# Splitting the first loads, doing the first projections chunk by chunk, warming TensorE with zeros, and merging the last segment's two projections

## The chip, the cores and the metric

The kernel runs on one core of one Trainium2 chip. The metric is the device time of one execution in microseconds (us); lower is better. A profile's span is about 1.7 us shorter than the time of the same execution. Five engines run side by side, each with its own instruction stream in order: TensorE (PE; its weight loads are listed as PEld), VectorE (DVE), ScalarE (ACT), GpSimd (POOL) and SyncE (SP). "ACTq" and "SPq" are the queues through which ScalarE and SyncE issue DMA transfers.

## The reference, cut to what matters

```python
# x: [1, 2048, 512] in 4 segments of 512 rows; 32 heads of width 16; all weights bf16
g = sigmoid((x * gate_w).sum(-1))
# A: causal attention inside each segment, plus a memory M, z summed over the earlier ones
q, k, v = x @ wq, x @ wk, x @ wv
o = sig(beta) * (phi(q) @ M) / (phi(q) @ z) + (1 - sig(beta)) * softmax(q k^T / 4 + mask) @ v
a = o @ wo
# B: a gated MLP, inner width 1792
b = (gelu(x @ w_gate) * (x @ w_up)) @ w_down
out = g * a + (1 - g) * b
```

## The kernel before

x is loaded transposed (`xT`, four chunks `fc` of 128 columns, each a partition block). A product of 512 rows with 128 weight columns is four matmuls of 128x128 by 128x512, accumulated in one PSUM bank. A list scheduler inside the kernel, fed with guesses of durations and of when loads arrive (`ext`), fixes each engine's order when the kernel is built. Its numbers are guesses, not measurements.

The loads and the guesses of their arrival (ns):

```python
load_w(nc.scalar, wk, A_wk)                 # whole, 512 KB, on ScalarE's queue
load_x(0)                                   # 4 transposing DMAs on SyncE's queue
load_w(nc.scalar, wq, A_wq)
load_w(nc.scalar, wv, A_wv)
nc.scalar.dma_start(gw[:, :], ...)
load_w(nc.scalar, wga, B_w_gate)            # 1792 KB
nc.scalar.dma_start(beta8[:, :], ...)
for s in range(1, NSEG): load_x(s)
load_w(nc.sync, wup, B_w_up); load_w(nc.sync, wdn, B_w_down); load_w(nc.sync, wo, A_wo)
a_x = [ext(t) for t in (7000, 11000, 16000, 20000)]
a_wk, a_wq, a_wv, a_gw = ext(5500), ext(8500), ext(11500), ext(12000)
```

k, then q, of segment 0, bank after bank (two `gen` banks in turn):

```python
def mm_x(t, W, c0, s):
    for fc in range(FC):
        nc.tensor.matmul(t, lhsT=W[:, fc, c0:c0 + P], rhs=xT[:, fc, s * L:(s + 1) * L],
                         start=(fc == 0), stop=(fc == FC - 1))
...
for c in range(NCH): qk_group(0, c, "k", 10 + c, "DVE")
for c in range(NCH): qk_group(0, c, "q", 20 + c, "DVE")
for kt in range(KT): v_group(0, kt, 30 + kt, "DVE")
```

The end of the last segment: the MLP product (`dn`) of each of four row blocks goes through a bank into dead space of `G`; the attention product (`fin`) has banks of its own; VectorE adds the two into one of two `osb` buffers, which are stored:

```python
def down_group(s, qt, prio):
    first, prev, box = pieces(s, qt, prio, True, ...)       # 14 matmuls, one bank
    ... copy(e, G[:, 0, qt, :], box["t"][:, :])             # evicted by ACT or DVE
def final(h):                                               # h = 0, 1: two row blocks each
    ... proj_o(box["t"][:, i, :], 3, 2 * h + i, range(3), True)   # heads' chunks 0..2
    ... proj_o(box["t"][:, i, :], 3, 2 * h + i, [3], False)       # the last chunk
    ... nc.vector.tensor_add(bx["o"][:, :], box["t"][:, i, :], G[:, 0, 2 * h + i, :])
    ... store(s, 2 * h + i, bx["o"])
```

The softmax here doesn't subtract the row's maximum and nothing guards it: scores larger than these inputs give would overflow.

## Time and profile before

| | before |
|---|---|
| time, median of all 15 runs beside the change | 299.29 us (the first three alone: 299.54) |
| span of the profiled run | 297.7 us |
| TensorE busy | 275.7 us, 93% |
| first k matmul | 7.60 us |
| first attention logits (`lg`) | 84.7 us |
| start of the last `pv` matmul | 274.8 us |

From the page's second part (the span in 40 slices of 7.4 us; a digit is the busy share in tenths, PEclk the granted clock in tenths):

```profile
PE   0999999999999979999998999998999999999991
PEclk9999999999999999999999999999999999999998
GB/s 194 205 320 277 308 3 0 2 0 0 0 2 36 6 39 30 36 2 2 1 2 35 20 53 20 20 1 2 0 21 21 18 2 18 20 21 18 20 0 70
```

TensorE is idle in the first slice and nearly so in the last; in all others it is busy for seven tenths or more. So those two are where most time can be had without doing less work. Note the granted clock: it reads 9 in every slice but the last. The next view shows why that isn't the whole truth.

From the timeline of before, its first 23 us (start, duration, engine, line, operation, out<-in, shape, count, and in brackets the idle time ahead and what ended it):

```profile
7.60 6.17 PE L314 MATMUL k<-xT,wk 128*128 128x512 bf16 x16 [7.60 <-DMA xT<-in_A_x_dram]
7.80 0.44 ACTq L239 DMA_DIRECT2D wv<-in_A_wv_dram  x1
8.41 0.15 PEld L314 LDWEIGHTS <-wk 128*128 128x128 bf16 x1 [0.28 <-issue]
8.84 0.15 PEld L314 LDWEIGHTS <-wk 128*128 128x128 bf16 x1 [0.28 <-issue]
12.68 0.60 PEld L314 LDWEIGHTS <-wk 128*128 128x128 bf16 x3 [0.28 <-issue]
13.00 0.44 ACTq L239 DMA_DIRECT2D wga<-in_B_w_gate_dram  x1
13.66 3.01 PE L314 MATMUL q<-xT,wq 128*128 128x512 bf16 x12
14.33 1.28 ACT L378 ACT_TABLE_LOAD   x1 [14.33 <-DMA gw<-in_gate_w_dram]
17.73 3.78 PE L352 MATMUL v<-wv,xT 128*128 128x512 bf16 x16
22.28 10.09 PE L314 MATMUL gt<-xT,wga 128*128 128x512 bf16 x46
```

TensorE waits for x until 7.60. Then the weight loads, one per matmul, start 0.43 us apart (8.41, 8.84) until 12.68; from there three take 0.60 us together, and later matmuls of this shape come 0.216 us apart. The array runs at half speed for its first 5.1 us of work, and the PEclk row doesn't show it. `wga`, which the gate matmuls (`gt`) need, is only issued at 13.00: ScalarE's queue stands still between its issues. The view doesn't name the reason; `wv` left at 7.80, after `wq` had landed (1.27 + 5.9 = 7.2), and `wga` at 13.00, after `wv` had (7.80 + 4.5 = 12.3), which fits issues that wait for an earlier load but doesn't show it. ScalarE's first work of its own, a table load, starts at 14.33, when the last issue is done.

From the DMA view of before, the last figure being the time from issue to landing:

```profile
wga<-in_B_w_gate_dram ACTq DMA_DIRECT2D x1, 1792.0 KB, 7.5
wk<-in_A_wk_dram ACTq DMA_DIRECT2D x1, 512.0 KB, 4.3
```

The tail of before, from the timeline:

```profile
290.12 1.03 PE L752 MATMUL fin<-wo,xT 128*128 128x512 bf16 x4
290.81 1.29 DVE L817 TENSOR_TENSOR osb<-fin,G 128x512 bf16<-128x512 f32 x2 [12.42 <-PE fin L752]
291.53 3.45 SPq L757 DMA_DIRECT2D out_dram<-osb  x4
293.33 1.29 DVE L817 TENSOR_TENSOR osb<-fin,G 128x512 bf16<-128x512 f32 x2 [1.24 <-DMA out_dram<-osb]
```

The last matmul ends at 290.12 + 1.03 = 291.15; 6.55 us follow. Two adds wait 1.24 us for a store to give an `osb` buffer back.

Two lines, from the views of the tiles `lg` and `pv`, divide the span ("84.7 to 264.0" are the first and last start):

```profile
L496 PE MATMUL lg<-qT,kT x320: 213/278/386, 84.7 to 264.0; 16*128 16x256 bf16 x64, 16*128 16x128 bf16 x64, 16*128 16x512 bf16 x32
L545 PE MATMUL pv<-pT,vz x640: 218/272/393, 99.6 to 274.8; 128*32 128x256 bf16 x64, 128*32 128x128 bf16 x64, 128*32 128x512 bf16 x32
```

I call what lies before the first `lg` the start (84.7 us), what lies between it and the last `pv` the middle (190.1), and the rest the end (22.9).

### The profile page before, as it was taken

To read this page: it belongs to the slowest core of one execution; us is meant where nothing else is said; L and a number is where in the kernel's file an instruction comes from. 1 tells how busy PE (TensorE), PEld (TensorE's weight loads), DVE (VectorE), ACT (ScalarE), POOL (GpSimd) and SP (SyncE) were. 2 spreads that over 40 slices of the span, in tenths; PEclk is the share of its full clock that TensorE was granted. 3 is DMA by queue.
4 is the path that set the end of the run, shared out by engine and by line. 5 is a ranking of instruction groups with operands and counts; after the bars stand their busy time and mean duration, and the time that the engine had idled before them with its cause. 6 is when DMAs were issued, how large, how long until landed. Compare 5 with 4: busy or idle time off the path is not lost.

```text
span 297.7 us, 5661 instructions
## 1 busy us (share of the span) xinstructions
PE 275.7 (93%) x2297; PEld 117.6 (40%) x2297; DVE 203.2 (68%) x361; ACT 206.7 (69%) x224; POOL 126.1 (42%) x186
## 2 busy tenths in 40 slices
PE   0999999999999979999998999998999999999991
PEld 0344444444433434344334444433444434344440
DVE  0484465446567798987999788689977855867303
ACT  0007565443479997899998899999998989984110
POOL 7000000000007883974558687564755864663000
PEclk9999999999999999999999999999999999999998
DMA  7998900000001011100001020000000000000002
GB/s 194 205 320 277 308 3 0 2 0 0 0 2 36 6 39 30 36 2 2 1 2 35 20 53 20 20 1 2 0 21 21 18 2 18 20 21 18 20 0 70
DMA packets 23106, 13.74 MB, mean 46 GB/s; under 512 B 16168, under 2 KB 22056, under 8 KB 23080
## 3 DMA queue, kind: packets, MB, share of 16 engines
q1 hardware_dynamic: 20400, 9.97, 12.1%
q10 hardware_dynamic: 2680, 3.41, 3.7%
q8 instruction: 18, 0.29, 0.4%
q14 instruction: 8, 0.07, 0.1%
HBM read 7.60 MB, written 2.10 MB: 33 GB/s over the span
## 4 chain that ended last, share of the span: by engine, by line
PE 73%; DVE 21%; DMA 3%; issue 1%; ACT 0%; DVEq 0%
PE gt L314 16%; PE dn L747 15%; PE up L314 14%; PE lg L496 6%; PE pv L545 5%; PE k L314 4%; PE v L352 3%; PE dn L752 3%; PE q L314 3%; DVE T L563 2%; DMA xT<-in_A_x_dram 2%; DVE G L416 2%; DVE Nm L736 2%; DVE N L581 2%; DVE Tm L732 1%; DVE vz L178 1%
## 5 line engine op out<-in xcount | busy, mean ns | idle before, releaser
L517 ACT ACTIVATE pT<-lg 128x1024 bf16<-128x1024 f32 x160 | 153.5, 1028 | 12.9 <-PE lg L496 12.3
L526 POOL TENSOR_SCALAR_AFFINE_SELECT pT<-pT 128x512 bf16<-128x512 bf16 (+1 forms) x160 | 94.4, 601 | 139.3 <-ACT pT L517 138.7
L416 DVE TENSOR_TENSOR G<-up,G 128x512 bf16<-128x512 f32 x56 | 38.3, 687 | 28.4 <-PE up L314 28.3
L314 PE MATMUL up<-xT,wup 128*128 128x512 bf16 x224 | 56.0, 380 | 0.6 <-DVE G L416 0.4
L747 PE MATMUL dn<-wdn,G 128*128 128x512 bf16 x224 | 53.3, 380 | 0.1
L314 PE MATMUL gt<-xT,wga 128*128 128x512 bf16 x224 | 51.0, 379 | 0.0
L404 ACT ACTIVATE G<-gt 128x1024 bf16<-128x1024 f32 x28 | 28.7, 1023 | 30.3 <-PE gt L314 30.3
L314 PEld LDWEIGHTS <-wga 128*128 128x128 bf16 x224 | 21.9, 98 | 26.5
L747 PEld LDWEIGHTS <-G 128*128 128x128 bf16 x224 | 20.2, 98 | 25.6 <-issue 4.1
L314 PEld LDWEIGHTS <-wup 128*128 128x128 bf16 x224 | 20.0, 97 | 25.8 <-issue 5.6
L563 DVE STREAM_TRANSPOSE T<-pv 128x512 f32<-128x512 f32 x32 | 22.7, 711 | 10.3 <-PE pv L545 10.3
L407 DVE TENSOR_TENSOR G<-G,g1b 128x1024 bf16<-128x1024 bf16 x28 | 19.2, 687 | 13.7 <-ACT G L404 13.7
L545 PE MATMUL pv<-pT,vz 128*32 128x256 bf16 (+2 forms) x640 | 23.4, 275 | 3.0 <-POOL pT L526 1.8
L314 PE MATMUL k<-xT,wk 128*128 128x512 bf16 x64 | 18.1, 427 | 8.6 <-DMA xT<-in_A_x_dram 7.6
L496 PE MATMUL lg<-qT,kO 32*128 32x128 bf16 (+2 forms) x320 | 18.1, 272 | 0.0
L496 PE MATMUL lg<-qT,kT 16*128 16x256 bf16 (+2 forms) x320 | 17.9, 274 | 0.0
L314 PE MATMUL q<-xT,wq 128*128 128x512 bf16 x64 | 16.3, 380 | 0.8 <-DVE kT L178 0.5
L545 PEld LDWEIGHTS <-vz 128*32 128x32 bf16 x640 | 12.6, 97 | 11.1 <-DVE G L416 2.2
L352 PE MATMUL v<-wv,xT 128*128 128x512 bf16 x64 | 15.7, 379 | 1.0 <-DVE vz L178 0.5
L618 POOL TENSOR_TENSOR pkT<-E,Q 128x1024 bf16<-128x1024 bf16 x6 | 13.5, 2254 | 3.6 <-DVE E L614 2.1
L581 DVE TENSOR_TENSOR N<-T,r 128x512 bf16<-128x512 f32 x16 | 14.8, 926 | 0.3
L496 PEld LDWEIGHTS <-kT 16*128 16x128 bf16 x320 | 7.1, 92 | 19.6 <-issue 19.2
(78 smaller groups left out, 240.4 us busy)
## 6 DMA issues: line engine op xcount, KB each, us to landing
out_dram<-osb SPq DMA_DIRECT2D x16, 128.0 KB, 1.7
wga<-in_B_w_gate_dram ACTq DMA_DIRECT2D x1, 1792.0 KB, 7.5
wup<-in_B_w_up_dram SPq DMA_DIRECT2D x1, 1792.0 KB, 7.4
wdn<-in_B_w_down_dram SPq DMA_DIRECT2D x1, 1792.0 KB, 13.3
wk<-in_A_wk_dram ACTq DMA_DIRECT2D x1, 512.0 KB, 4.3
wq<-in_A_wq_dram ACTq DMA_DIRECT2D x1, 512.0 KB, 5.9
wv<-in_A_wv_dram ACTq DMA_DIRECT2D x1, 512.0 KB, 4.5
wo<-in_A_wo_dram SPq DMA_DIRECT2D x1, 512.0 KB, 14.1
```

The lines of the kernel that those rows point to most:

```text
L314: nc.tensor.matmul(t, lhsT=W[:, fc, c0:c0 + P], rhs=xT[:, fc, s * L:(s + 1) * L], start=(fc == 0), stop=(fc == FC - 1))
L352: nc.tensor.matmul(t[:, :], lhsT=xT[:, fc, s * L + kt * P:s * L + (kt + 1) * P], rhs=wv[:, fc, :], start=(fc == 0), stop=(fc == FC - 1))
L404: ge = evac("ACT", g, box, lambda e, t: nc.scalar.activation(dst, t[:, :, :], AF.Gelu_apprx_tanh), cost=960, ring="lg")
L407: GM[(s, hp)] = add("DVE", 620, lambda e: nc.vector.tensor_mul(dst, dst, g1b[:, s * L:(s + 1) * L][:, None, :].to_broadcast((P, 2, L))), d ...
L416: UPT[(s, hs)] = evac("DVE", g, box, lambda e, t: nc.vector.tensor_mul(G[:, s, hs, :], t[:, :], G[:, s, hs, :]))
L496: nc.tensor.matmul(A[j // 2][:, j % 2, at * P:(at + nq) * P], lhsT=l, rhs=r, start=True, stop=True, tile_position=(32 * j, 0))
L517: nc.scalar.activation(pT[(s, t, h)][:, :, :], A[h][:, :, :], AF.Exp, scale=0.25)
L526: nc.gpsimd.affine_select(out=v, in_=v, pattern=pat, compare_op=ALU.is_ge, fill=0.0, base=0, channel_multiplier=-1)
L545: nc.tensor.matmul(t[32 * j:32 * j + 32, qb * P:(qb + nq) * P], lhsT=vz[s % 2][:, kt, h * VW:h * VW + 32], rhs=pT[(s, t0 + w, j // 2)][:, ...
L563: nc.vector.transpose(TT[key][:, e, :, :].rearrange("p a b -> p (a b)"), t[:, :])
L581: nc.vector.tensor_mul(NN[key][:, :, :, :].rearrange("p a e d -> p e a d"), TT[key][:, :, :, 0:DH], RR[key][:, :, :, :].to_broadcast((P, 2 ...
L747: nc.tensor.matmul(t[:, :], lhsT=G[:, s, hs, qt * P:(qt + 1) * P], rhs=wdn[:, hs, :], start=(hs == 0), stop=stop and (hs == HS - 1))
```

## The change

Its intent is to let TensorE begin earlier and warm, and to shorten what follows its last matmul. The diff, cut to its core:

```diff
-    load_w(nc.scalar, wk, A_wk)
+    warm = p1.tile([P, L], BF, name="warm", tag="warm")
+    nc.vector.memset(warm[:, :], 0.0)
     load_x(0)
-    load_w(nc.scalar, wq, A_wq)
-    load_w(nc.scalar, wv, A_wv)
-    nc.scalar.dma_start(gw[:, :], ...)
-    load_w(nc.scalar, wga, B_w_gate)
-    nc.scalar.dma_start(beta8[:, :], ...)
+    for h in range(2):
+        nc.scalar.dma_start(wk[:, 2 * h:2 * h + 2, :], wkr[:, 2 * h:2 * h + 2, :])
+    for h in range(2):
+        nc.scalar.dma_start(wq[:, 2 * h:2 * h + 2, :], wqr[:, 2 * h:2 * h + 2, :])
+    load_w(nc.sync, wv, A_wv)
+    nc.sync.dma_start(wga[:, :, 0:4 * P], wgr[:, :, 0:4 * P])
+    nc.sync.dma_start(wga[:, :, 4 * P:DFF], wgr[:, :, 4 * P:DFF])
     for s in range(1, NSEG):
         load_x(s)
+    nc.sync.dma_start(gw[:, :], ...)
+    nc.sync.dma_start(beta8[:, :], ...)
...                                   # new arrival guesses, gw at 27000 instead of 12000
-    for c in range(NCH): qk_group(0, c, "k", 10 + c, "DVE")
-    for c in range(NCH): qk_group(0, c, "q", 20 + c, "DVE")
+    first_qk()
...
+    def first_qk():
+        ...
+            t = lgtile("warm")
+            for i in range(9):
+                nc.tensor.matmul(t[:, 0, :], lhsT=warm[:, 0:P], rhs=warm[:, :], start=True, stop=True)
+        ...                           # eight banks: 3 lg tiles of two banks, 2 gen banks
+        for fc in range(FC):
+            for n, W in (("k", wk), ("q", wq)):
+                def fn(_, fc=fc, n=n, W=W):
+                    for c in range(NCH):
+                        nc.tensor.matmul(banks[(n, c)], lhsT=W[:, fc, c * P:(c + 1) * P],
+                                         rhs=xT[:, fc, 0:L], start=(fc == 0), stop=(fc == FC - 1))
...
-            down_group(s, qt, nx())            # and final(0), final(1)
+    for qt in range(KT):
+        out_group(NSEG - 1, qt, 9000 + qt)     # dn and wo projection in one bank, one copy, one store
```

The new TensorE order is: nine matmuls on zeros, k0 k1 k2 q0 q1 k3 q2 q3 (chunks of four matmuls each), one gate pair, half of v, one gate pair, the rest of v, six gate pairs, and only then the gate row, because `gw` is loaded late. From the first `lg` to shortly before the last `pv` the order is as before.

More of the change, by code (lines that the diff above doesn't have):

```diff
@@ L244 @@
     g1b = p1.tile([P, NSEG * L], BF, name="g1b", tag="g1b")
-    load_w(nc.scalar, wk, A_wk)
-    load_x(0)
-    load_w(nc.scalar, wq, A_wq)
-    load_w(nc.scalar, wv, A_wv)
-    nc.scalar.dma_start(gw[:, :], gate_w.rearrange("(fc p) -> p fc", p=P))
-    load_w(nc.scalar, wga, B_w_gate)
-    nc.scalar.dma_start(beta8[:, :], A_beta.rearrange("(c h) -> h c", h=8))
+    warm = p1.tile([P, L], BF, name="warm", tag="warm")
+    nc.vector.memset(warm[:, :], 0.0)
+    wkr = A_wk.rearrange("(fc p) n -> p fc n", p=P)
+    wqr = A_wq.rearrange("(fc p) n -> p fc n", p=P)
+    wgr = B_w_gate.rearrange("(fc p) n -> p fc n", p=P)
+    load_x(0)
+    for h in range(2):
[5 more added lines that the diff above has]
+    nc.sync.dma_start(wga[:, :, 4 * P:DFF], wgr[:, :, 4 * P:DFF])
     for s in range(1, NSEG):
         load_x(s)
+    nc.sync.dma_start(gw[:, :], gate_w.rearrange("(fc p) -> p fc", p=P))
+    nc.sync.dma_start(beta8[:, :], A_beta.rearrange("(c h) -> h c", h=8))
     load_w(nc.sync, wup, B_w_up)
@@ L260, in ext @@
         return add("EXT", 0, lambda e: None, lat=at)
-    a_x = [ext(t) for t in (7000, 11000, 16000, 20000)]
-    a_wk, a_wq, a_wv, a_gw = ext(5500), ext(8500), ext(11500), ext(12000)
-    a_wga, a_be, a_wup, a_wdn, a_wo = ext(19000), ext(20000), ext(28000), ext(33000), ext(35000)
+    a_x0 = [ext(t) for t in (3300, 4900, 6100, 7300)]
+    a_x = [a_x0[3], ext(18000), ext(22000), ext(26000)]
+    a_wk0, a_wq0 = ext(4000), ext(7000)
+    a_wk, a_wq = a_wk0, a_wq0
+    a_wv, a_gw = ext(9000), ext(27000)
+    a_wg0, a_wga, a_be, a_wup, a_wdn, a_wo = [ext(t) for t in
+                                              (10500, 14000, 27500, 32000, 37000, 39000)]
     nc.gpsimd.memset(oddj[:, :], 1.0)
@@ L315, in mm_x, with odd_copy, fo @@
                              start=(fc == 0), stop=(fc == FC - 1))
+    def odd_copy(s, c, ev):
+        pr = c // 2
+        ko = ("o", s, pr)
+        def fo(e):
+            if ko not in QK:
+                QK[ko] = rtile("kO", [P, 2, L])
+            nc.vector.tensor_scalar_mul(QK[ko][:, c % 2, :], QK[("k", s, pr)][:, c % 2, :],
+                                        odd[:, :])
+        new = ko not in first_ev
+        o = add("DVE", 400, fo, prio=2, deps=[ev] + ([] if new else [first_ev[ko]]),
+                alloc=["kO"] if new else [])
+        first_ev.setdefault(ko, o)
+        EVQK[("o", s, c)] = o
     def qk_group(s, c, which, prio, engs):
@@ L336, in qk_group @@
         if which == "k":
-            ko = ("o", s, pr)
-            def fo(e):
-                if ko not in QK:
-                    QK[ko] = rtile("kO", [P, 2, L])
-                nc.vector.tensor_scalar_mul(QK[ko][:, c % 2, :], QK[key][:, c % 2, :], odd[:, :])
-            new = ko not in first_ev
-            o = add("DVE", 400, fo, prio=2, deps=[ev] + ([] if new else [first_ev[ko]]),
-                    alloc=["kO"] if new else [])
-            first_ev.setdefault(ko, o)
-            EVQK[("o", s, c)] = o
+            odd_copy(s, c, ev)
@@ new lines, in first_qk, with f_warm, f_open, fe @@
+    def first_qk():
+        tl = {}
+        banks = {}
+        def f_warm(_):
+            t = lgtile("warm")
+            for i in range(9):
+                nc.tensor.matmul(t[:, 0, :], lhsT=warm[:, 0:P], rhs=warm[:, :],
+                                 start=True, stop=True)
+        w = add("PE", 3800, f_warm, prio=0, alloc=["lg"])
+        free_w = add("EXT", 0, lambda _: None, deps=[w], frees=[("lg", w)])
+        def f_open(_):
+            for i in range(3):
+                tl[i] = lgtile("qk0")
+            for n in "kq":
+                for pr in range(2):
+                    QK[(n, 0, pr)] = rtile(n + "T", [P, 2, L])
+            for c in range(NCH):
+                banks[("k", c)] = tl[c // 2][:, c % 2, :]
+            for c in range(2):
+                banks[("q", c)] = tl[2][:, c, :]
+                banks[("q", 2 + c)] = gen("qk0")[:, :]
+        op = add("PE", 1, f_open, prio=0, deps=[w], alloc=["lg", "lg", "lg", "gen", "gen",
+                                                          "kT", "kT", "qT", "qT"])
+        last = {}
+        for fc in range(FC):
+            for n, W in (("k", wk), ("q", wq)):
+                def fn(_, fc=fc, n=n, W=W):
+                    for c in range(NCH):
+                        nc.tensor.matmul(banks[(n, c)], lhsT=W[:, fc, c * P:(c + 1) * P],
+                                         rhs=xT[:, fc, 0:L], start=(fc == 0), stop=(fc == FC - 1))
+                last[n] = add("PE", 4 * MM, fn, prio=1 + fc + (0 if n == "k" else 1.5),
+                              deps=[op, a_x0[fc], a_wk0 if n == "k" else a_wq0])
+                read_x[0].append(last[n])
+        for n, ring in (("k", "kT"), ("q", "qT")):
+            for c in range(NCH):
+                pr = c // 2
+                key = (n, 0, pr)
+                first_ev[key] = op
+                fr = [(("lg", pr), op)] if n == "k" else (
+                    [(("lg", 2), op)] if c < 2 else [(("gen", c - 2), op)])
+                engs = ["DVE", "ACT"]
+                def fe(e, n=n, c=c, key=key):
+                    copy(e, QK[key][:, c % 2, :], banks[(n, c)])
+                EVQK[(n, 0, c)] = add(engs, [EV[e] for e in engs], fe, prio=0, deps=[last[n]],
+                                      frees=fr)
+                if n == "k":
+                    odd_copy(0, c, EVQK[(n, 0, c)])
@@ L400, in mms @@
                 mm_x(t[:, i, :], wga, (2 * hp + i) * P, s)
-        g, box = group("gt", 8 * MM, mms, prio, [a_x[s], a_wga], alloc="lg")
+        g, box = group("gt", 8 * MM, mms, prio, [a_x[s], a_wg0 if hp < 2 else a_wga], alloc="lg")
         read_x[s].append(g)
@@ L440, in f_wo @@
             nc.vector.tensor_scalar_mul(wo[:, c, :], wo[:, c, :], omg[:, c:c + 1])
-    for c in range(NCH):
-        qk_group(0, c, "k", 10 + c, "DVE")
-    for c in range(NCH):
-        qk_group(0, c, "q", 20 + c, "DVE")
+    first_qk()
     for kt in range(KT):
@@ L510, in logit_slot @@
             frees = [(n + "T" if n != "o" else "kO", first_ev[(n, s, pr)]) for n in "qko"]
+            if s == 0:
+                frees = [((r, pr) if r != "kO" else r, x) for r, x in frees]
         g = add("PE", 240, fn, prio=0, deps=deps, mode="row", alloc=["lg", "lg"], frees=frees,
@@ L766, in fn @@
                 if lo == 0:
-                    box["t"] = gen("dn")
+                    box["t"] = lgtile("dn")[:, 0, :] if s == NSEG - 1 and qt == 0 else gen("dn")
                 down(box["t"], s, qt, lo, hi, last)
@@ L770, in pieces @@
                        deps=(hd + [a_wdn] + list(deps)) if lo == 0 else [prev],
-                       alloc=["gen"] if lo == 0 else [])
+                       alloc=["lg" if s == NSEG - 1 and qt == 0 else "gen"] if lo == 0 else [])
             first = first or prev
@@ L775, in out_group @@
     def out_group(s, qt, prio):
-        first, prev, box = pieces(s, qt, prio, False,
-                                  [t_wo] + [OTT[(s, c)] for c in range(NCH)])
+        ott = [OTT[(s, c)] for c in range(NCH)]
+        swap = s == NSEG - 1 and qt == 0
+        first, prev, box = pieces(s, qt, 3999 if swap else prio, False,
+                                  [t_wo] + ([XT_[(NSEG * NSLOT - 1, 1)]] if swap else ott))
         g = add("PE", 4 * MM, lambda _: proj_o(box["t"][:, :], s, qt, range(NCH), False), prio=prio,
-                deps=[prev])
+                deps=[prev] + ott)
         bx = {}
@@ L785, in out_group @@
         ev = add(["DVE", "ACT"], [610, 560], fn, prio=0, deps=[g], alloc=["osb"],
-                 frees=[("gen", first)])
+                 frees=[("lg" if s == NSEG - 1 and qt == 0 else "gen", first)])
         OUTE[(s, qt)] = ev
         add("SP", 600, lambda _: store(s, qt, bx["o"]), deps=[ev], frees=[("osb", ev)], lat=2000)
-    def down_group(s, qt, prio):
-        first, prev, box = pieces(s, qt, prio, True, [OUTE[(0, q)] for q in range(KT)])
-        OUTE[("dn", qt)] = add(["DVE", "ACT"], [610, 560],
-                               lambda e: copy(e, G[:, 0, qt, :], box["t"][:, :]), prio=0,
-                               deps=[prev],
-                               frees=[("gen", first)])
-    def final(h):
-        box = {}
-        def f0(_):
-            box["t"] = lgtile("fin")
-            for i in range(2):
-                proj_o(box["t"][:, i, :], NSEG - 1, 2 * h + i, range(3), True)
-        def f1(_):
-            for i in range(2):
-                proj_o(box["t"][:, i, :], NSEG - 1, 2 * h + i, [3], False)
-        s = NSEG - 1
-        a = add("PE", 6 * MM, f0, prio=1e4 + h, deps=[t_wo] + [OTT[(s, c)] for c in range(3)]
-                + [XT_[(NSEG * NSLOT - 1, 1)]], alloc=["lg"])
-        b = add("PE", 2 * MM, f1, prio=1e4 + 2 + h, deps=[a, OTT[(s, 3)]])
-        for i in range(2):
-            bx = {}
-            def fe(e, i=i, bx=bx):
-                bx["o"] = rtile("osb", [P, D])
-                nc.vector.tensor_add(bx["o"][:, :], box["t"][:, i, :], G[:, 0, 2 * h + i, :])
-            ev = add("DVE", 610, fe, deps=[b, OUTE[("dn", 2 * h + i)]], alloc=["osb"],
-                     frees=[("lg", a)])
-            add("SP", 600, lambda _, i=i, bx=bx: store(s, 2 * h + i, bx["o"]), deps=[ev],
-                frees=[("osb", ev)], lat=2000)
     TAB["first_x"] = None
@@ L870, in fillers @@
                 out_group(*long.pop(0), nx())
-        if s == NSEG - 1:
-            for qt in range(KT):
-                down_group(s, qt, nx())
     for s in range(NSEG):
@@ L886 @@
                 pv_group(s, c, 1)
-    for h in range(2):
-        final(h)
+    for qt in range(KT):
+        out_group(NSEG - 1, qt, 9000 + qt)
     S.run()
```

## The prediction

> **What bounds the kernel now.** TensorE: busy 275.7 of 297.7 us (the page's first part). By stretches (the windows view): nothing until 7.6 us; projections at a poor rate to 22.3; gate and up matmuls without a gap to 84.85; attention to 278, with VectorE (157 of 193 us) and ScalarE (172) loaded as well; then matmuls, evictions and stores. The change touches the first 22 us and the last 20.
>
> **Start.** The first matmul waits for xT until 7.60 (the chain of waits begins with that DMA). The transposes of segment 0, issued 1.25 us apart from 0.80, land at about 7.6 to 8.8, behind all of wk (4.3 us) and mixed with wq. Then k is slow: the timeline's weight loads come every 0.427 us until 12.7, every 0.216 later. The Trainium skill, "TensorE: Matmul & The Clock Gate", Part 1, says a cold array runs at half rate until about 3.4 us of sustained activity; the spacings agree, the 5.1 us here is longer. k, q, v and the gate row take 14.7 us for 52 matmuls, at 0.216 they are 11.2.
>
> After: nine matmuls on zeros (9 x 0.427 = 3.8 us, about 1.2 to 5.1) warm the array while loads fly; k and q accumulate chunk by chunk in eight banks, starting on the first chunk of x and half of wk. I estimate that chunk at 5.0 to 6.5 us, the last at 8.5. 32 x 0.216 = 6.9 us: q ends near 13.0 (14.5 if the clock isn't up) instead of 17.9. At the 300 to 400 GB/s seen from 15 to 20 us, wv and wga arrive before use (near 11 and 16; use from 13 and 20). gw lands last, near 27; the gate row is moved to near 30. VectorE, 53% busy there, catches up the late g1b multiplies. Gain: 4.4 us, nearly all critical, as TensorE then has no gap until 84.85.
>
> **Middle.** TensorE's order in the attention stage is unchanged: 193 us, give or take 0.7.
>
> **Tail.** Before: the last matmul ends near 291.15, then two adds, two more that wait for a free osb (1.2 us on a store), and stores: 6.5 us to the end. After: down and output projection accumulate in one bank, group by group, with the same number of matmuls; only the last group's copy and store follow. From the last eviction's end to the end of the span was 3.1 us: 0.2 + 0.6 + 3.1 = 3.9. Gain 2.6 us; fin's wait for xT near 271 (0.3 us) goes too: 2.9.
>
> **Sum.** 299.54 - 4.4 - 2.9 = 292.2 us, range 290.2 to 294.8. Faster by over 2%: 0.74; within 2%: 0.25; slower: 0.01.
>
> **What would show it.** First k matmul at 5 to 6.5 us; nearly no 0.427 spacing after the warm ones; q done by 13 to 14.5; first attention logits near 80.5 instead of 84.9; no TensorE gap for wga or gw; one osb copy of 0.6 us after the last matmul, under 4.2 us from there to the end.
>
> **What would make it wrong.** x0's first chunk still landing after 7 us; the clock dropping after the warm matmuls, or not yet up (up to 2.5 us); gw or wo so late that VectorE, which runs in order, holds up an eviction; eight banks' evictions delaying the first gate pair or v; the start's gain being eaten in the attention stage, where buffers recur in rings.

## The result

The median went from 299.29 us (15 runs, 298.48 to 301.05) to 292.06 us (12 runs, 291.09 to 293.07). The ratio is 0.9762, 95% interval 0.9744 to 0.9779. A ratio here is the mean time of one kernel's fast runs over that of the other's of the same rounds, so not quite the ratio of the medians. Of the experiments' runs two of before's (303.11 and 303.93 us) were slow and are left out of the ratios.

Fast runs of one kernel differ too. Of the change's twelve, the three with a granted clock of 0.994 took 292.86 to 293.07 us; the nine with 0.998 or 1.000 took 291.09 to 292.53.

The first stretch of the changed kernel, from its timeline:

```profile
1.25 4.02 PE L373 MATMUL warm<-warm 128*128 128x512 bf16 x9 [1.25 <-DVE warm L247]
6.08 4.60 PE L396 MATMUL qk<-xT,wk 128*128 128x512 bf16 x12 [0.81 <-DMA xT<-in_A_x_dram]
6.89 0.15 PEld L396 LDWEIGHTS <-wk 128*128 128x128 bf16 x1 [0.28 <-issue]
7.32 0.15 PEld L396 LDWEIGHTS <-wk 128*128 128x128 bf16 x1 [0.28 <-issue]
7.18 0.51 SPq L258 DMA_DIRECT2D wga<-in_B_w_gate_dram  x1
9.87 0.32 PEld L396 LDWEIGHTS <-wk 128*128 128x128 bf16 x2 [0.28 <-issue]
12.88 1.09 ACT L176 ACTIVATE kT<-qk 128x512 bf16<-128x512 f32 x2 [7.12 <-PE qk L396]
14.84 1.89 PE L326 MATMUL gt<-xT,wga 128*128 128x512 bf16 x8
16.56 1.89 PE L420 MATMUL v<-wv,xT 128*128 128x512 bf16 x8
21.74 10.52 PE L326 MATMUL gt<-xT,wga 128*128 128x512 bf16 x48
```

x's first chunk came at about 6.0 instead of 7.6, and `wga` is issued by 7.18 instead of 13.00. But the zeros ended at 5.27, TensorE was idle for 0.81 us, and the k matmuls still came 0.43 us apart until 9.87. Nine of them were slow. In this run the zeros had not warmed the array by the time they ended.

Its tail:

```profile
286.56 1.03 PE L819 MATMUL dn<-wo,xT 128*128 128x512 bf16 x4
287.67 0.60 ACT L176 ACTIVATE osb<-dn 128x512 bf16<-128x512 f32 x1 [3.29 <-PE dn L819]
288.29 0.33 SPq L824 DMA_DIRECT2D out_dram<-osb  x1
```

One copy and one store remain; from the last matmul's end (287.59) to the end of the span (290.8) it is 3.2 us. The dividing lines and the slices:

```profile
L561 PE MATMUL lg<-qT,kT x320: 212/278/385, 81.6 to 260.9; 16*128 16x256 bf16 x64, 16*128 16x128 bf16 x64, 16*128 16x512 bf16 x32
L612 PE MATMUL pv<-pT,vz x640: 219/272/392, 96.5 to 270.9; 128*32 128x256 bf16 x64, 128*32 128x128 bf16 x64, 128*32 128x512 bf16 x32
PE   7999999999999979999998999998999999999995
PEclk9999999999999999999999999999999999999999
```

The start lost 3.1 us (84.7 to 81.6), the middle 0.8 (190.1 to 189.3), the end 3.0 (22.9 to 19.9): 6.9 us, the whole difference of the spans. That the slow spacing of the k matmuls leaves no mark in PEclk can be seen in both kernels. About 0.5 us of the end's 3.0 goes with the loads and not with the tail; see start_only.

### The profile page after: what moved, and what is told of

Its sections match the earlier page's. It is cut to its first block, busy times and chain, and to the rows that moved or that the text cites. A ratio compares the mean times of both kernels' runs of the same rounds, so it can differ in the third digit from the quotient of the medians.

```text
span 290.8 us, 5680 instructions
## 1 busy us (share of the span) xinstructions
PE 278.2 (96%) x2306; PEld 118.9 (41%) x2306; DVE 197.1 (68%) x354; ACT 208.7 (72%) x228; POOL 126.1 (43%) x186
## 4 chain that ended last, share of the span: by engine, by line
PE 76%; DVE 20%; DMA 2%; issue 1%; ACT 1%; ACTq 0%
PE gt L326 17%; PE dn L814 16%; PE up L326 15%; PE lg L561 6%; PE pv L612 6%; PE dn L819 4%; PE v L420 3%; PE qk L396 3%; PE q L326 3%; DVE T L630 2%; DVE N L648 2%; DVE G L484 2%; PE k L326 2%; DMA xT<-in_A_x_dram 2%; DVE Nm L803 2%; DVE Tm L799 1%
## 5 line engine op out<-in xcount | busy, mean ns | idle before, releaser
L326 PEld LDWEIGHTS <-wga 128*128 128x128 bf16 x224 | 21.8, 98 | 26.2
L475 DVE TENSOR_TENSOR G<-G,g1b 128x1024 bf16<-128x1024 bf16 x28 | 18.3, 681 | 1.8 <-ACT G L472 1.8
L176 ACT ACTIVATE osb<-dn 128x512 bf16<-128x512 f32 x9 | 5.4, 596 | 17.5 <-PE dn L819 17.5
L819 PE MATMUL dn<-wo,xT 128*128 128x512 bf16 x64 | 16.3, 380 | 0.0
```

The costliest lines, as they stand in the source:

```text
L819: nc.tensor.matmul(t, lhsT=xT[:, c, s * L + qt * P:s * L + (qt + 1) * P], rhs=wo[:, c, :], start=first and c == 0, stop=(c == NCH - 1))
```

## The experiments

My theory was: the start gains because x's first chunk arrives earlier and can be used at once, and the zeros take the slow stretch out of the critical path; the end gains because fewer evictions and stores follow the last matmul. Rivals: one of the three parts of the start does it all (loads, chunk order, zeros); the zeros do nothing; the gain of the middle belongs to the start. Twelve runs were made in three jobs, ten new kernels and two repeats; each job ran on one chip beside the kernel before, whose medians there were 299.26, 299.08 and 299.32 us. All gave correct results.

| run | first k, us | slow k/q matmuls | first lg | middle | end | median, us | ratio to before |
|---|---|---|---|---|---|---|---|
| before | 7.60 | 12 | 84.7 | 190.1 | 22.9 | 299.29 | 1 |
| the change | 6.08 | 9 | 81.6 | 189.3 | 19.9 | 292.06 | 0.9762 |
| tail_only | 7.21 | 11 | 84.6 | 189.2 | 20.5 | 295.60 | 0.9860 |
| start_only | 5.78 | 2 | 81.0 | 190.1 | 22.3 | 295.18 | 0.9866 |
| no_warm | 5.66 | 11 | 81.9 | 189.2 | 20.0 | 292.83 | 0.9770 |
| warm12 | 6.34 | 1 | 80.9 | 189.2 | 20.0 | 292.06 | 0.9753 |
| old_loads | 7.54 | 7 | 91.4 | 189.2 | 20.5 | 302.29 | 1.0087 |
| new_loads | 6.08 | 14 | 84.6 | 189.2 | 20.0 | 295.74 | 0.9873 |
| q_early | 5.74 | 0 | 80.2 | 189.2 | 20.0 | 291.48 | 0.9737 |
| quarters | 6.34 | 1 | 81.2 | 190.4 | 20.7 | 293.40 | 0.9795 |
| chunk_old | 7.64 | 8 | 85.2 | 190.1 | 22.9 | 300.25 | 1.0033 |
| warm_and_G | 7.57 | 0 | 84.6 | 190.1 | 21.5 | 297.83 | 0.9951 |
| change_again | 5.46 | 4 | 80.4 | 189.2 | 20.0 | 291.62 | 0.9745 |
| q_early_again | 6.20 | 0 | 80.2 | 189.2 | 20.0 | 291.17 | 0.9727 |

The columns up to "end" are from one profile each; slow matmuls are counted from the 0.43 us spacing of weight loads, give or take one. The middle is the last `pv` start less the first `lg`, the end is the span less the last `pv`. "The loads" are several edits at once (halves of `wk` and `wq`; x ahead of `wk` in the program; `wv`, `wga`, `gw` on SyncE's queue; `gw` last); no run tells them apart.

### tail_only: the new tail alone

Edit: the last part of the diff above on the kernel before, nothing of the start.

> The kernel before with only the new tail (down and output projection in one bank, group by group). My theory: independent of the start; from the last matmul to the end 6.5 us become 3.8, and the 0.3 us wait of fin for xT goes: 2.8 to 3.7 us less than before, so about 296. Rival: the 0.9 us that the attention stage lost in the profile of the change belongs to the new start (another phase of the buffer rings); then here only 2.5 to 2.8 us, and the stage from first logits to last pv stays 189.6 us.

Measured 295.60 us (294.81 to 296.06), 3.66 us below before's median in its job; ratio 0.9860, interval 0.9818 to 0.9902. The first `lg` stayed at 84.6; the middle shrank to 189.2 and the end to 20.5. So the middle's 0.9 us belongs to the tail edit and not to the start: that rival falls. The tail, from its timeline:

```profile
289.55 1.03 PE L752 MATMUL dn<-wo,xT 128*128 128x512 bf16 x4
290.66 0.60 ACT L176 ACTIVATE osb<-dn 128x512 bf16<-128x512 f32 x1 [3.29 <-PE dn L752]
```

From the last matmul's end (290.58) to the end of the span (294.3) it is 3.7 us, where I expected 3.8. Part of the middle's 0.9 is plain bookkeeping. Before the last `pv`, the old order has 6 `fin` and 10 `dn` matmuls, the new one 14 `dn`: two matmuls (0.43 us) moved behind it, from the middle into the end. In the old order the `fin` matmuls also waited 0.28 us for VectorE's `xT`.

### start_only: the new start alone

Edit: the rest of the diff, with `down_group` and `final` kept.

> The kernel before with only the new loads, the nine matmuls on zeros and the chunk-by-chunk k and q. Theory: first logits near 81.6 instead of 84.75, and all of that kept: 3.0 to 4.0 us less than before, with the tail as before (6.5 us after the last matmul). The sum of this gain and tail_only's should be the 7 us of the whole change. Rival (the parts need each other): the sum misses 7 us by more than 1.

Measured 295.18 us (one run of six at 297.81), 4.08 below before; ratio 0.9866. The middle is as before (190.1), but the end is 0.6 shorter (22.3) with the old tail: from the end of the last eviction to the end of the span it is 2.5 us here and 3.1 before. In all eight profiles with the change's loads this last stretch is 2.5 to 2.6 us, in the other six (loads as before, and quarters) 3.0 to 3.3, whatever the tail. The last store lands 1.7 us after its issue in both kinds (before, tail_only, quarters; the change, start_only, q_early). So about 0.5 us of the gain at the end belongs to the loads. Why isn't shown. Gains of 3.66 and 4.08 add up to 7.7, against 7.2 for the whole change and 7.7 for it in the third job (299.32 to 291.62): the two halves are independent within the spread. The run of 297.81 had the lowest granted clock of the six (0.986, the others 0.994 to 0.997).

In this profile only two k matmuls were slow, with the same nine zeros and a gap of 0.50 us behind them. The clock's rise isn't fixed from run to run.

### no_warm and warm12: what the zeros do

Edits on the change:

```diff
 # no_warm                                   # warm12
-            for i in range(9): matmul(...)    -            for i in range(9):
+            pass                              +            for i in range(12):
```

> The changed kernel without its nine matmuls on zeros, all else in the same order. Theory A ([...]in the profile of the change the 0.8 us gap before the first k matmul threw the warming away: 9 k matmuls still came 0.427 us apart): 10 to 14 slow k matmuls here instead of 9, so 0.2 to 1.0 us slower than the change. Rival B (the nine matmuls did their job in most runs): 14 to 16 slow ones against few, 2 to 2.5 us slower.

> The changed kernel with 12 matmuls on zeros instead of 9, so that they run until about 6.4 us, past the arrival of the first chunk of x (6.04). Theory A (a gap threw the warming away): the clock rises during the zeros or within four k matmuls; at most 4 slow k matmuls; q ends near 13.7 instead of 15.0; 0.7 to 1.4 us faster than the change. Rival B (the gap does not matter, the rise comes by itself at some time): again about 9 slow k matmuls and 0 to 0.4 us slower than the change.

Measured in one job: 292.83 us without zeros (291.96 to 293.54), 292.06 with twelve (291.79 to 293.53). The medians differ by 0.8 us but the ranges overlap. Each has one run at a granted clock of 0.994 (293.54 and 293.53); without these two the ranges are 291.96 to 292.95 and 291.79 to 292.10, which still touch. The profiles point the same way: 11 slow matmuls and first `lg` at 81.9 without, one and 80.9 with twelve. Weight loads of warm12, from its timeline:

```profile
5.91 0.15 PEld L396 LDWEIGHTS <-wk 128*128 128x128 bf16 x1 [0.28 <-issue]
6.34 0.15 PEld L396 LDWEIGHTS <-wk 128*128 128x128 bf16 x1 [0.28 <-issue]
6.77 1.45 PEld L396 LDWEIGHTS <-wk 128*128 128x128 bf16 x7 [0.28 <-issue]
8.93 1.02 PE L396 MATMUL qk<-xT,wk 128*128 128x512 bf16 x4 [0.43 <-DMA xT<-in_A_x_dram]
```

From 6.77 on, seven loads take 1.45 us: the array is fast. And at once the next limit shows: TensorE waits 0.43 us for x's third chunk, which arrives at 8.9. So here the zeros can't save the 2.3 us that eleven slow matmuls cost; twelve of them save about 1 us, and then the load of x binds. Rival B (2 to 2.5 us) falls. That zeros make fewer matmuls slow is shown by more profiles: 8 to 14 slow ones in the five without zeros, none or one in the five with twelve or fifteen. That this is worth 0.8 us rests on the medians above; two profiles of the same kernel differ by more (below).

Two points went against me. I expected twelve zeros to be 0.7 to 1.4 us faster than nine; warm12 and the change have the same median, 292.06, though from different jobs. And twelve zeros are both more and without a gap ahead of k, so these runs don't tell whether it was the gap that threw the warming away: in warm_and_G a gap of 0.58 us follows fifteen zeros and no matmul is slow.

### old_loads: new compute order, loads as before

Edit: the change with the load statements of the kernel before.

> The changed kernel with the loads as before (all of wk, then wq, wv, gw, wga on the ScalarE queue, whole), computing chunk by chunk after nine zero matmuls. Theory (the early arrival of x's first chunk, 5.7 to 6.1 us against 7.2 to 7.6, comes from the halved weights): first k matmul at 7.2 to 7.8 again, warming lost in a gap of 2 us, so 10 to 14 slow k matmuls; q done near 16.5 to 17; 1.2 to 2.2 us slower than the change. Rival (chunk-by-chunk order alone brings the gain): no more than 0.5 us slower.

Measured 302.29 us, 10.2 above the change (in another job) and slower than before (1.0087, interval 1.0050 to 1.0125). I expected 1.2 to 2.2. The main cause isn't x but `wga`. From its timeline:

```profile
7.54 4.12 PE L393 MATMUL qk<-xT,wk 128*128 128x512 bf16 x12 [2.27 <-DMA xT<-in_A_x_dram]
21.82 3.59 PE L323 MATMUL gt<-xT,wga 128*128 128x512 bf16 x8 [5.84 <-DMA wga<-in_B_w_gate_dram]
```

k and q are done near 16, but the new order puts a gate pair next, and its weights arrive at 21.8. TensorE, which runs in order, stands for 5.84 us with v ready to go behind it, and after that gap it starts slow again: eight matmuls take 3.59 us, against 1.89 in the change. This time the page of the run shows it too:

```profile
PEclk9986999999999999999999999999999999999999
```

This run confounds two things, the loads and an order made for other loads; it shows that the order is only as good as the arrival times it was built for. chunk_old, below, is the cleaner test.

### new_loads: new loads, k and q bank after bank, no zeros

Edit: `first_qk()` replaced by the old `qk_group` calls; the rest of the change kept.

> The changed kernel with its loads, but k and q of segment 0 bank after bank as before and no zero matmuls. The first bank's second chunk and third wait for x as it arrives (6.9, 8.5, 8.8 us), so TensorE can only do 3 matmuls before 8.5 and is cold until about 11 to 12. Theory: q done near 17, 1.5 to 2.5 us slower than the change, so that chunk order and split loads each bring little without the other. Rival (the loads alone bring it): under 0.7 us slower than the change.

Measured 295.74 us: 3.7 above the change, and the first `lg` at 84.6, as before. From its timeline:

```profile
6.99 0.59 PE L326 MATMUL k<-xT,wk 128*128 128x512 bf16 x1 [0.33 <-DMA xT<-in_A_x_dram]
8.63 5.92 PE L326 MATMUL k<-xT,wk 128*128 128x512 bf16 x14 [1.05 <-DMA xT<-in_A_x_dram]
```

A bank needs all four chunks in turn, so TensorE does single matmuls between waits, and the bulk starts at 8.63, slow. The new loads without chunk order and zeros give the start nothing (0.1 us). I had expected a loss of 1.5 to 2.5 us against the change and underestimated it.

### chunk_old: chunk order alone

Edit: the kernel before with `first_qk` (no zeros), old loads, old tail; the old guesses, but for new ones for x's four chunks. `first_qk` also lets ScalarE evict k and q, which only VectorE did before.

> The kernel before with its own loads and tail; only the k and q of segment 0 are done chunk by chunk in eight banks, with no zeros and without moving wv, wga or the gate row behind gate pairs (old_loads had that confounded: its gate pairs were put before loads that came later). Theory (chunk order pays only when chunks arrive early): x's chunks land together near 7.2 to 8.8 us, the array is cold for 10 to 12 matmuls, q done near 16.5 to 17.2 instead of 17.9: 0.3 to 1.4 us less than before. Rival (chunk order brings most of the start's gain): 2.5 us or more less than before.

Measured 300.25 us, 0.9 above before (ratio 1.0033, interval 1.0010 to 1.0056): slightly slower, where I expected a gain of 0.3 to 1.4. From its timeline:

```profile
14.33 1.28 ACT L176 ACT_TABLE_LOAD   x1 [14.33 <-DMA gw<-in_gate_w_dram]
15.62 1.57 ACT L176 ACTIVATE kT<-qk 128x512 bf16<-128x512 f32 x3
18.23 3.84 PE L407 MATMUL v<-wv,xT 128*128 128x512 bf16 x16 [1.92 <-ACT qT L176]
```

Chunk order fills eight banks at once, and five of the eight evictions go to ScalarE here. ScalarE's stream still holds all the load issues up to `beta` ahead of them, so its first eviction starts at 15.62, and v waits 1.92 us for a free bank. In the changed kernel, where `wv`, `gw` and `wga` are on SyncE's queue, ScalarE's evictions start at 12.88. So moving those loads isn't an aside: with them on ScalarE's queue and the evictions shared with ScalarE, the chunk order didn't pay. Whether it would with all evictions on VectorE was not run. And without that wait the gate matmuls, which start at 21.91 here, could have begun near 20.0, before `wga` landed (13.02 + 7.5 = 20.5), so some of it would have been lost to the next limit.

### warm_and_G: zeros alone at the start, no `osb` wait at the end

Edits on the kernel before, one at each end:

```diff
+    wt = lgtile("warm")
+    for i in range(15):
+        nc.tensor.matmul(wt[:, 0, :], lhsT=warm[:, 0:P], rhs=warm[:, :], start=True, stop=True)
...
-                bx["o"] = rtile("osb", [P, D])
+                bx["o"] = G[:, 1, 2 * h + i, :]       # rows that are dead by then
...                                                 # and the store reads bx["o"] from there
```

> The kernel before with two small edits, told apart by the stretch of the profile they act on: 15 matmuls on zeros ahead of the first k (from 1.25 to about 7.6 us), and the last four adds write into dead rows of G instead of osb, so that none waits for a store. Theory: the zeros bridge to the arrival of x, so the 12 slow k matmuls become 0 to 2 and the first logits come 1.5 to 2.4 us earlier (VectorE's evictions of k take 0.69 + 0.35 us per bank and may then bind); after the last matmul 6.5 us become 5.2. Together 2.6 to 3.6 us less than before. Rival for the tail (the two pairs of adds and not the osb wait are what costs): the tail shrinks by under 0.5 us.

Measured 297.83 us (ratio 0.9951, interval 0.9929 to 0.9972), 1.5 below before; I expected 2.6 to 3.6. The ends are told apart by the profile. At the start the zeros did what they should: no slow matmul, v begins at 15.82 instead of 17.73. And all of it was given back:

```profile
22.10 2.12 PE L319 MATMUL gt<-xT,wga 128*128 128x512 bf16 x9 [1.56 <-DMA wga<-in_B_w_gate_dram]
290.64 2.48 DVE L822 TENSOR_TENSOR G<-fin,G 128x512 bf16<-128x512 f32 x4 [12.44 <-PE fin L757]
```

TensorE waits 1.56 us for `wga`, and the gate matmuls start at 22.10 (22.28 before). The late `wga` was a second limit close behind the first. It landed at 22.1 here, 1.6 us later than in the profile of before; at 20.5 it would have taken almost nothing. That isn't shown to be the zeros' doing: in tail_only, whose start is the old one, it landed at 22.1 as well, and the first gate weights waited 0.63 us for it. At the end the four adds now run in one go (2.48 us) and the end is 21.5 us instead of 22.9: 1.4 us is what the wait for `osb` cost, as expected. From the last matmul to the end it is 5.2 us, against 6.55 before and 3.7 in tail_only. The step from 5.2 to 3.7 is one copy in place of four adds: the adds end 2.15 us after the last matmul, the copy 0.68. The change's own profile has 3.2 because of the shorter last stretch that goes with its loads.

### q_early, quarters, and the repeats

q_early has twelve zeros and the order k0 k1 q0 q1 k2 q2 k3 q3:

```diff
-        for fc in range(FC):
-            for n, W in (("k", wk), ("q", wq)):
+        for n, fc in (("k", 0), ("k", 1), ("q", 0), ("q", 1), ("k", 2), ("q", 2), ("k", 3), ("q", 3)):
```

quarters adds eight loads of 128 KB in that order to it, instead of four of 256 KB.

> 12 zero matmuls, and the chunks of q pulled ahead: k0 k1 q0 q1 k2 q2 k3 q3. In warm12 the clock was up at 6.8 us and TensorE then idled 0.4 us for x's third chunk (8.93). Theory (the third chunk of x is what bounds the start once the clock is up): no wait there, q done near 13.2 to 13.6 instead of 14.1, 0.5 to 0.9 us faster than warm12, near 291.4. Rival: the half of wq arrives late as well and the wait only moves.

> As q_early, with wk and wq loaded in quarters of 128 KB in the order of use, so that fewer weight bytes stand between the chunks of x. Theory (x's chunks are held up by the weight halves that share the DMA engines): first chunk of x at or below 5.5 us, third below 8.0; all 32 matmuls without a wait from 6.4 on; equal to q_early or up to 0.5 us faster. Rival (small transfers cost more than they save, the last quarter comes late): slower than q_early by 0.3 to 1 us, with a wait before k3 or q3.

> The changed kernel once more, beside q_early_again on the same chip. Expected 292.1 us, give or take 0.5, with 2 to 11 slow k matmuls, as the moment at which the clock rises is not fixed.

> q_early once more beside the change: if 12 zeros and the early q are a real gain, 0.4 to 1.2 us less than change_again; if the difference between the earlier jobs was the chip, under 0.3 us.

q_early: 291.48 us, ratio 0.9737; 0.6 us below warm12 of another job, as expected. The wait for x's third chunk is gone. From the timeline of q_early_again:

```profile
6.20 1.89 PE L398 MATMUL qk<-xT,wk 128*128 128x512 bf16 x8
7.93 1.89 PE L398 MATMUL qk<-xT,wq 128*128 128x512 bf16 x8
9.65 1.03 PE L398 MATMUL qk<-xT,wk 128*128 128x512 bf16 x4
```

On one chip beside the change: 291.17 us (four runs, 291.09 to 291.31) against 291.62 (five, 291.29 to 292.10). All nine had a granted clock of 0.998 or 1.000. The 0.45 us is at the lower edge of what I expected (0.4 to 1.2) and the intervals against before overlap (0.9703 to 0.9751, 0.9720 to 0.9771). q_early is probably the better version, by about half a microsecond; it is shown only as far as these runs go.

quarters lost: 293.40 us, 1.9 above q_early in the same job, where even the rival had said 0.3 to 1. Its last quarter of wq arrived late and q3 waited for it until 13.59 us (0.65 us). That start is still earlier than the first profile of the change had; its profiled run was also 1.2 us longer in the middle and 0.7 in the end than q_early, where nothing was edited. The page shows a mark in the middle:

```profile
PEclk9999999999999998999999999999999999999999
```

The windows view gives a granted clock of 0.78 from 108 to 110 us, 0.50 from 110 to 112 and 0.86 from 112 to 114, and 1.00 around that. Matmuls on `wk` and `wq` there take longer than in q_early: from the first of them to the next `lg` after the block of four q, 4.7 us against 3.5. So the middle's 1.2 us is a dip of the clock in that one execution and not the edit's. The 0.7 at the end is the last stretch named under start_only (3.25 against 2.6 us). What set off the dip isn't shown.

The change's first profile (nine slow matmuls, first `lg` 81.6) and its second (four, 80.4) differ by 1.2 us with the same code. This is part of the spread of its runs, and more than the zeros are worth by the medians.

## Why the prediction was right

It said 292.2 us, range 290.2 to 294.8; 292.06 was measured. Point by point:

- **Which ends of the span would give, and the middle not:** right. The middle gave 0.8 us, at the rim of the 0.7 I allowed, and tail_only shows that it comes from the tail edit.
- **Start, 4.4 us:** 3.1 in the profile beside the result, 4.3 in the repeat, 3.7 in start_only. First chunk at 5.0 to 6.5 us: about 6.0. Loads of `wv` and `wga` in time: no wait for them. First logits near 80.5: 81.6 and 80.4.
- **"Nearly no 0.427 spacing after the warm ones":** wrong in that profile, nine slow matmuls; four and two in others. q was done by about 15.0 (the last q matmuls start at 13.11 and take 1.89), outside the 13 to 14.5 that I named. The prediction did list "or not yet up (up to 2.5 us)" as a risk. no_warm and warm12 put the whole matter at about 1 us, because x's third chunk binds when the clock is up. So the step "the zeros warm the array" failed in the result's own profile and held in part in the others.
- **Tail, 2.9 us:** right in mechanism and nearly in size. In tail_only the time from the last matmul to the end fell from 6.55 to 3.7 us (3.9 was estimated), 2.8 us; with the 0.28 us wait of `fin` that makes 3.1 of the 3.4 by which its span is shorter. Its start gave 0.1; some 0.2 us I can't assign. The medians say 3.66.
- **The sum was closer than its terms, and that was luck.** In the result's own profile the start gave 1.3 us less than I said, and middle and end together 0.9 more (3.8). About 0.5 of that 0.9 is the shorter last stretch that goes with the new loads, which I didn't foresee.
- **What I didn't see:** why the parts need each other. I counted the later arrival of x and the slow clock as the start's costs, as if taking them away had to show. The start's gains in the first `lg`, against 84.7 and from one profile each: new loads alone 0.1, chunk order alone -0.5, zeros alone 0.1, loads and chunk order together 2.8, all three 3.1 to 4.3. Behind the wait for x stood `wga` (zeros alone), behind the loads stood the order of banks (new_loads), behind the order stood ScalarE's queue, with ScalarE sharing the evictions (chunk_old).

## What to carry to other kernels

When a stretch has several limits close behind one another, an edit that removes only the first can show nothing; write down when each later operand arrives and when it is needed, and remove all the limits that lie within the expected gain. Load issues on an engine that must also evict PSUM can delay its first eviction (15.62 us in chunk_old, 12.88 in the change), so try them on a queue whose engine has nothing else to do. Count matmul spacing to see a slow TensorE, and if you warm it with dummy work, make that work long enough: nine zeros left two to nine slow matmuls, twelve or fifteen left none or one. Before you explain a difference of 1 us between two profiles, compare their granted clocks window by window.

## What the Trainium skill lacked or had wrong

- "TensorE: Matmul & The Clock Gate", Part 1, says that the rise comes around 4 us into sustained activity, give or take 0.5 us, and also that the window runs free, so that the count of slow matmuls varies. Here it took longer or shorter: in these profiles the unbroken time from the first matmul to the fast spacing was 3.3 us (chunk_old), 3.8 (q_early), 5.1 (before) and 5.5 (warm12): the spread is wider than the first figure, and the second statement is the one to go by. Nine slow k matmuls, four, or two followed the same nine zeros.
- The same page says that idle time of about a 3.4 us window throttles the array. It doesn't say what a short gap does to a warming that isn't finished: after gaps of 0.81, 0.50 and 0.19 us behind the zeros, the array was still slow for 3.8, 1.1 and about 1.7 us. After 2.27 us (old_loads) it was slow for 2.9, so the length of the gap alone doesn't order them. The free window may explain it; no run here settles it.
- No page that I read says that the profile's granted clock reads 9 tenths or more while matmuls come 0.43 instead of 0.216 us apart (before, 7.6 to 12.7 us; in the windows view it is 1.00 there, and also while TensorE is still idle before 7.6). A fall after a gap of 5.84 us does show there (old_loads, 8 and 6 tenths in the third and fourth slice), and so does the dip of quarters, 0.50 from 110 to 112 us.
- "DMA: Bandwidth & Descriptors", section "Issuing engines are not separate DMA queues", says that issuing from several engines only saves the issuing sequencer's time, usually small. What it can cost when the issuing engine has work of its own is missing: with six loads on its queue, ScalarE's first work started at 14.33 us (before, chunk_old), and its late evictions stopped TensorE for 1.92 us.
